# The head of a linear-attention and MLP kernel: the first key weight chunk loaded ahead of the second tile of tokens, and the first tile started alone

## The chip, the cores and the metric

The kernel runs on one core of a Trainium2 chip. A core has TensorE (PE, matrix products; PEld is its loading of weights), VectorE (DVE), ScalarE (ACT), GpSimd (POOL) and SyncE (SP, here a queue that issues DMA transfers), each with its own stream of instructions, in order, and semaphores between them. On-chip memory is SBUF, 128 partitions wide; TensorE writes its results into PSUM. The metric is the time of one execution in microseconds on the device, lower is better. Before the change the median of 3 runs is 414.81 us (414.78 to 414.87).

## The reference

Tokens x (2048 rows, 512 wide, float32) are normalised per row and go through two branches that are added to x:

```python
xn = _layernorm(x, axis=-1)
return x + _A_ref(xn, A_wqkv, A_wo) + _B_ref(xn, B_w1, B_b1, B_w2, B_b2)
```

Branch A is linear attention with 32 heads of 16: q, k and v are `xn @ wqkv`; `phi(t)` is `t + 1` above 0 and `exp(t)` below, plus 1e-6; per head `kv = phi(k)^T v` and `z = sum phi(k)`; the output is `(phi(q) kv) / (phi(q) z + 1e-6)`, times `wo`. Branch B is `relu(xn w1 + b1)^2 w2 + b2` with 1376 hidden units. The row normalisation is

```python
m = jnp.mean(x, axis=axis, keepdims=True)
v = jnp.var(x, axis=axis, keepdims=True)
return (x - m) / jnp.sqrt(v + eps)
```

The change touches only this normalisation and the key product `xn @ wk` of the first two tiles.

## The kernel before

The 2048 tokens are 16 tiles of 128. A float32 product is made of three passes: each operand is split into a high part (`h`, rounded) and a low part (`l`, the rest), and high by high, low by high and high by low are added in PSUM. The key weights `wk` are four chunks of 128 rows (`rk` as loaded, `wk[0]` high, `wk[1]` low), so the keys of a tile take 4 x 3 = 12 products of 128x512. For the first two tiles these products stand in an order written out by hand, since tokens and weights are still arriving.

A tile goes through these steps:

- `load_x` (line 159): its tokens by DMA on SP.
- `measure` (lines 230, 231): two DVE operations give mean and variance.
- `roots`: DVE adds eps to the variance (line 241), POOL raises it to the power -0.5 (line 242).
- `normalise`: DVE subtracts the mean and multiplies by the root, giving `xp` (line 264).
- `transposed` / `turned_pe`: four TensorE turns (line 304) into PSUM, as two halves of two chunks each for tiles 0 and 1. `high()` then has ScalarE round a half into `xs1h` (line 320), and `low()` has DVE subtract that from the PSUM half, giving `xs1l` (line 323). Behind the turns, POOL's memset (line 342) writes 1 into the last column of `xp`.
- `some(i, u, js)` (line 365) issues the products of tile i's part u (0 high, 1 low) with the high parts of weight chunks js, and `rest(j)` those of both tiles' high parts with the low part of chunk j.
- Later `phi_k` makes phi of the keys (lines 356 to 360), `tokens` splits the normalised tokens (ScalarE, then POOL at line 119), `parts` splits the keys (ScalarE, then DVE at line 373), and `kx` (line 385) multiplies the two and adds into four PSUM banks over all tiles.

`heads_k(j)` copies chunk j of the key weights on ScalarE to its high part (line 111, `wkh`), and `rests_k(engine, j)` subtracts that from the chunk on DVE or POOL (line 559, `wkl`). POOL does chunk 1, DVE chunks 0, 2 and 3.

No planner orders this. The program is written under a manual schedule: every engine does its instructions in the order of the Python text, and waits at each for what it needs. So moving a line moves its instruction past others of its own engine. SP's queue holds, in this order, tile 0, tile 1, the four key chunks, tiles 2 and 3 (one transfer), and tiles 4 to 7 (`x4`, one transfer). The last is held back by a small POOL copy out of `xp` of tile 1 into `x4` (line 586). Eleven products of zeros run on TensorE while the first loads are under way.

Behind the head the work is a steady alternation of keys (12 products of line 365), turns (4) and `kx` (12 products of line 385), and then the products of queries, attention and the MLP by tiles of the hidden units.

Of the kernel before, what the change touches and what calls it, by code (L numbers as in the profile page):

```python
# [10 lines left out]
OP = mybir.AluOpType  # L11
# [7 lines left out]
def kernel(  # L19
# [30 lines left out]
    nc = tc.nc  # L50
# [5 lines left out]
    NJ = D // P  # L56
# [24 lines left out]
    def w512(name, tag, bufs):  # L81
        return work.tile([P, 512], F32, name=name, tag=tag, bufs=bufs)
# [8 lines left out]
    def two(name):  # L91
        return keep.tile([P, 2, 512], F32, name=name, tag=next_tag("x"))

    def four(name, tag, dt=F32, pool=None):
        return (pool or work).tile([P, TB, 512], dt, name=name, tag=tag)
# [4 lines left out]
    def f32(ap):  # L100
        return ap.bitcast(F32)

    def gjc(ap):

        return ap.rearrange("p (j g c) -> p g j c", j=NJ, g=NJ)
# [3 lines left out]
    def copy(eng, o, i, bias=0.0):  # L109
        if eng == "act":  # L110
            nc.scalar.activation(o, i, AF.Copy, bias=bias)  # L111
        elif bias:
            ENG[eng].tensor_scalar(o, i, bias, None, op0=OP.add)
        else:
            ENG[eng].tensor_copy(o, i)
# [41 lines left out]
    def load_x(i, t):  # L157
        n = t.shape[1]
        nc.sync.dma_start(t, xf[i * P:(i + n) * P, :].rearrange("(i p) d -> p i d", i=n))
        for k in range(n):  # L160
            xr[i + k] = t[:, k]
# [6 lines left out]
    def chunk(w, j, a, b):  # L168

        return w[j * P:(j + 1) * P, a:b]  # L170
# [52 lines left out]
    def group(*tiles):  # L223
        return tiles, *(small.tile([P, 3, k], F32, name=f"{n}{tiles[0]}", tag=n) for n, k in (("st", 6), ("mv", 2), ("y", 3)))

    def measure(g, *ks):

        tiles, st, mv, _ = g
        for k in ks or range(len(tiles)):
            nc.vector.bn_stats(st[:, k, :], xr[tiles[k]])  # L230
            nc.vector.bn_aggr(mv[:, k, :], st[:, k, :])

    def statistics(*tiles):
        g = group(*tiles)
        measure(g)
        return g

    def roots(tiles, st, mv, y):

        n = len(tiles)  # L240
        nc.vector.tensor_scalar(y[:, 1, :n], mv[:, :n, 1], 1e-5, None, op0=OP.add)
        nc.gpsimd.tensor_tensor(out=y[:, 0, :n], in0=y[:, 1, :n], in1=power[:, :n], op=OP.pow)  # L242

    def normalise(tiles, st, mv, y):

        n = len(tiles)
        r, u = (y[:, k, :n] for k in range(2))
        if tiles[-1] >= NPE:

            nc.vector.scalar_tensor_tensor(u, mv[:, :n, 0], -1.0, r, op0=OP.mult, op1=OP.mult)  # L250
        later = []

        def last(i, o, src, k):
            nc.scalar.activation(o, src, AF.Identity, bias=u[:, k:k + 1], scale=r[:, k:k + 1])
            if i in groups:
                regroup(i)

        for k, i in enumerate(tiles):
            o, src = xp[i], xr[i]
            if i >= NDVE:  # L260

                o, src = o.rearrange("p g (j c) -> p g j c", j=NJ), gjc(src)
            if i < NPE:
                nc.vector.tensor_scalar(o, src, mv[:, k, 0:1], r[:, k:k + 1], op0=OP.subtract, op1=OP.mult)
                if i in groups:
                    regroup(i)
            else:
                later.append(lambda a=(i, o, src, k): last(*a))
        return later
# [3 lines left out]
    def regroup(i):  # L273

        src, G = groups[i]
        via = dram.tile([P, NJ, src.shape[-1]], F32, name=f"via{i}")
        nc.sync.dma_start(via, src)
        of_g = via.rearrange("(r t) g n -> g t r n", r=NJ)
        for g in range(NJ):
            moves.append((G[32 * g:32 * (g + 1)], of_g[g]))  # L280
# [6 lines left out]
    def turn(o, G):  # L287

        nc.vector.transpose(o.rearrange("p j (r t) -> p r j t", r=NJ),
                            G.rearrange("p r (j c) -> p r j c", j=NJ))  # L290

    def slot(i):
        return slice((i % TB) * P, (i % TB + 1) * P)

    def cols(i):

        return xsb[(i // TB + 1) % 2]

    def turned_pe(i, n=1):

        t = [bank(f"pt{i}{k}", "acc" if i < 3 else "ps")[:, :D // n] for k in range(n)]
        for j in range(NJ):
            k, at = divmod(j * P, D // n)
            nc.tensor.transpose(t[k][:, at:at + P], xp[i][:, j * P:(j + 1) * P], ident)  # L304
        ones(i)
        return [p.rearrange("p (j t) -> p j t", j=NJ // n) for p in t]

    def transposed(i, n=1):

        b, at = i // TB, slot(i)  # L310
        if i < NDVE:
            t = turned_pe(i, n)
        else:
            t = [xT[b][:, :, at] if i >= NPE else w512(f"t{i}", "p", 6).rearrange("p (j t) -> p j t", j=NJ)]
            turn(t[0], xg[i])
        m = NJ // n
        h, l = ([x[:, k * m:(k + 1) * m, at] for k in range(n)] for x in cols(i))

        def high(k=0):
            nc.scalar.activation(h[k], t[k], AF.Copy)  # L320

        def low(k=0):
            nc.vector.tensor_tensor(out=l[k], in0=t[k], in1=f32(h[k]), op=OP.subtract)

        def keep_t():
            o = t[0]
            if i < NDVE:
                o = w512(f"t{i}", "p", 6).rearrange("p (j t) -> p j t", j=NJ)
                for k in range(n):
                    copy("act", o[:, k * m:(k + 1) * m], t[k])  # L330
            if i < NPE:
                nc.sync.dma_start(xTd[b][:, :, at], o)

        return high, low, keep_t
# [27 lines left out]
    def project(i, ps, w, steps, first=True, last=True):  # L362

        for n, (j, u, v) in enumerate(steps):
            nc.tensor.matmul(ps, lhsT=cols(i)[u][:, j, slot(i)], rhs=w[v][:, j, :], start=first and n == 0,  # L365
                             stop=last and n == len(steps) - 1)
# [147 lines left out]
    for _ in range(WARM):  # L514
        nc.tensor.matmul(pw[:, :P], lhsT=zeros, rhs=zeros, start=True, stop=True)
    t, rk = two("x0"), four("rk", "r0")
    for i in range(2):
        load_x(i, t[:, i:i + 1])
    def load_k(*js):
        for j in js:  # L520
            nc.sync.dma_start(rk[:, j], chunk(wqkv, j, D, 2 * D))

    load_k(*range(NJ))
    load_x(2, two("x2"))
    nc.gpsimd.memset(power, -0.5)
    nc.gpsimd.memset(ident, 0.0)
# [10 lines left out]
    for i0 in range(0, NT, TB):  # L537
# [5 lines left out]
        n = TB if i0 >= NPE else NPE - NDVE  # L543
        o = work.tile([P, n, 512], F32, name=f"xg{i0}", tag="r0" if i0 + TB == NT else "r3" if i0 >= NPE else "rc")
        for k in range(0, n, 2):
            i = i0 + TB - n + k
            u, v = (t.rearrange("p a (g c) -> p (a g c)", g=NJ) for t in (a[:, TB - n + k:][:, :2], o[:, k:k + 2]))
            groups[i + 1] = [t.rearrange("p (g n) -> p g n", g=NJ) for t in (u, v)]
            u, v = (t.rearrange("p (g i c) -> p g i c", g=NJ, i=2) for t in (u, v))
# [3 lines left out]
    def heads_k(*js, eng="act"):  # L553
        for j in js:
            copy(eng, wk[0][:, j, :], rk[:, j])

    def rests_k(eng, *js):
        for j in js:
            ENG[eng].tensor_tensor(out=wk[1][:, j, :], in0=rk[:, j], in1=f32(wk[0][:, j, :]), op=OP.subtract)
# [3 lines left out]
    def some(i, u, js, first=False):  # L563
        project(i, pks[i], wk, [(j, u, 0) for j in js], first, False)

    def rest(j):
        for i in range(2):
            project(i, pks[i], wk, [(j, 0, 1)], False, j == NJ - 1)

    two_tiles = group(0), group(1)  # L570
    for t in two_tiles:
        measure(t)
        roots(*t)
    normalise(*two_tiles[0])
    heads_k(0)
    high, low, keep0 = transposed(0, 2)
    normalise(*two_tiles[1])
    high1, low1, keep1 = transposed(1, 2)
    high()
    rests_k("dve", 0)  # L580
    some(0, 0, (0,), True)
    high1()
    low()
    some(0, 1, (0,))

    nc.gpsimd.tensor_copy(x4[:, 0, :1], xp[1][:, :1])
    load_x(4, x4)
    low1()
    some(1, 0, (0,), True)
    some(1, 1, (0,))  # L590
    rest(0)
    heads_k(1)
    rests_k("pool", 1)
    high(1)
    some(0, 0, (1,))
    some(0, 1, (1,))
    some(1, 0, (1,))
    some(1, 1, (1,))
    high1(1)
    rest(1)  # L600
    heads_k(2, 3)
    low(1)
    low1(1)
    third = statistics(2)
    roots(*third)
    rests_k("dve", 2)
    for j in (2, 3):
        for i in range(2):
            for u in range(2):
                some(i, u, (j,))  # L610
    normalise(*third)
    keep0()
    keep1()
# [2 lines left out]
    high, low, keep2 = transposed(2)  # L616
    high()
    low()
    rest(2)
    rest(3)  # L620
    load_x(8, x8[:, :2])
# [8 lines left out]
    parts(0)  # L630
    keep2()
    roots(*fourth)
    normalise(*fourth)
    phi_k(1, pks[1])
# [142 lines left out]
    for i in range(2, NT):  # L777
# [9 lines left out]
        high = low = keep_t = lambda: None  # L787
        if i + 1 < NDVE:
            high, low, keep_t = transposed(i + 1)
# [109 lines left out]
    for n in range(2):  # L899
# [339 lines left out]
        for e, f in enumerate(waiting[:-2]):  # L1239
# [14 lines left out]
            if n == 0 and 1 <= e < 5:  # L1254
                k, u = divmod(e - 1, 2)
# [68 lines left out]
```

## Time and profile before

| | |
|---|---|
| median of 3 runs | 414.81 us (414.78 to 414.87) |
| profiled execution, its own time | 414.74 us |
| span in the profile | 413.0 us |
| granted TensorE clock | 1.00 |
| TensorE busy | 407.2 us, 99% |
| VectorE busy | 311.9 us, 76% |
| ScalarE busy | 265.8 us, 64% |
| GpSimd busy | 55.8 us, 14% |
| TensorE busy from 0 to 8.93 us | 6.48 us |
| TensorE busy from 8.93 to 12.57 us | 3.64 us |
| TensorE busy from 12.57 to 20.20 us | 7.52 us |

A row of the timeline gives start, duration, engine, line, operation, the tile written and the tiles read, shapes, and in brackets how long the engine had been idle and what ended that. `x2` at the end of a row means that several instructions are merged, and the duration is theirs together. All times count from the start of the span. A row with `x` is the raw tokens, `xp` the normalised, `pt` the turned tokens in PSUM, `rk`, `wkh` and `wkl` the key weights, `pk` the keys, `y` the variance and its root, and `mv` the mean and variance. In the view of waits a row gives who waited for whom, the sum in us, how often, and the longest.

### The profile page before, as it was taken

The page shows a single profiled execution, that of the slowest core. Times are in us where ns is not written, and L with a number is a line of the kernel's source. Part 1 is how long each engine was busy: PE and PEld are TensorE (multiplying, and loading weights), DVE is VectorE, ACT ScalarE, POOL GpSimd, SP SyncE. Part 2 cuts the span into 40 slices and gives each one's busy share as a digit, 9 for nine tenths or more (in the row PEclk, how much of TensorE's full clock was granted, in tenths as well). Part 3 has the DMA queues.
Part 4 walks back from the last instruction along what each step waited for, and adds up shares of the span by engine and source line. Part 5 has one row for each costly group of instructions (what it writes and reads, how often), then busy time and mean ns, then how long its engine had stood idle before and what let it go on. Part 6 is the DMA issues. An engine that isn't in the chain of part 4 may idle for free.

```text
span 413.0 us, 5389 instructions
## 1 busy us (share of the span) xinstructions
PE 407.2 (99%) x1835; PEld 336.7 (82%) x1835; DVE 311.9 (76%) x563; ACT 265.8 (64%) x467; POOL 55.8 (14%) x81
## 2 busy tenths in 40 slices
PE   7999999999999999999999999999999999999996
PEld 6788888888888888888878888888888888878885
DVE  5795666798799898998439996468989685449843
ACT  4667667756678789788547631567588857737420
POOL 4442333220320000020000040100000200000310
PEclk9999999999999999999999999999999999999999
DMA  6889572710322312264267992411121781024502
GB/s 222 297 242 358 196 238 102 232 51 2 103 75 55 100 51 70 85 188 67 102 244 247 378 202 76 127 52 51 53 76 27 226 185 48 2 87 166 103 1 102
DMA packets 44925, 54.62 MB, mean 132 GB/s; under 512 B 7905, under 2 KB 29153, under 8 KB 43618
## 3 DMA queue, kind: packets, MB, share of 16 engines
q1 hardware_dynamic: 42594, 50.09, 36.9%
q0 software_dynamic: 2304, 4.20, 6.5%
q8 instruction: 14, 0.23, 0.2%
q14 instruction: 13, 0.11, 0.1%
HBM read 41.16 MB, written 13.11 MB: 131 GB/s over the span
## 4 chain that ended last, share of the span: by engine, by line
PE 96%; DVE 2%; DMA 1%; ACT 0%; POOL 0%; issue 0%
PE acc L130 37%; PE b L484 32%; PE kx L385 10%; PE pk L365 10%; PE acc L495 2%; PE pz L130 1%; PE pkv L875 1%; PE pm L130 1%; DMA x<-in_A_x_dram 1%; PE pz0b L130 1%; PE b L130 1%; DVE st L230 0%; POOL y L242 0%; PE acc L502 0%; PE pt L304 0%; DVE k L360 0%
## 5 line engine op out<-in xcount | busy, mean ns | idle before, releaser
L130 PE MATMUL acc<-w2r,s 128*128 128x512 f32 x477 | 112.8, 390 | 0.0
L130 PEld LDWEIGHTS acc<-w2r,s 128*128 128x128 f32 x477 | 89.5, 188 | 19.2 <-issue 0.7
L484 PE MATMUL b<-T,aop 128*128 128x512 f32 x336 | 83.4, 390 | 0.0
L484 PEld LDWEIGHTS b<-T,aop 128*128 128x128 f32 x336 | 63.1, 188 | 13.1
L385 PE MATMUL kx<-pk,tok 128*128 128x512 f32 x192 | 46.5, 392 | 0.1
L385 PEld LDWEIGHTS kx<-pk,tok 128*128 128x128 f32 x192 | 35.8, 188 | 7.7 <-ACT pk L111 0.4
L1005 POOL DMA_DIRECT2D res<-in_B_b_dram x16 | 14.2, 1069 | 182.6 <-DVE dt L426 64.7
L484 PE MATMUL b<-xs0h,aop 128*128 128x512 f32 x112 | 36.9, 391 | 0.0
L130 PE MATMUL acc<-mh,aTsr 128*128 128x512 f32 x112 | 35.7, 390 | 0.0
L1013 DVE TENSOR_TENSOR res<-acc,res 128x512 f32<-128x512 f32 x16 | 11.0, 692 | 23.1 <-PE acc L130 18.5
L119 POOL TENSOR_TENSOR tok<-xp,tok 128x512 fp32r<-128x512 f32 x16 | 20.8, 1303 | 43.5 <-ACT tok L111 43.5
L122 DVE TENSOR_TENSOR w2r<-r,w2r 128x512 fp32r<-128x512 f32 (+2 forms) x35 | 25.6, 734 | 0.1
L130 PEld LDWEIGHTS acc<-mh,aTsr 128*128 128x128 f32 x112 | 21.0, 188 | 4.4
L484 PEld LDWEIGHTS b<-xs0h,aop 128*128 128x128 f32 x112 | 21.0, 188 | 4.3
L111 ACT ACTIVATE aop<-S 128x512 fp32r<-128x512 f32 x28 | 17.5, 624 | 10.6 <-DVE S L704 10.6
L119 DVE TENSOR_TENSOR aop<-S,aop 128x512 fp32r<-128x512 f32 x28 | 19.5, 698 | 4.8 <-ACT aop L111 4.4
L119 DVE TENSOR_TENSOR s<-c,s 128x512 fp32r<-128x512 f32 x20 | 13.6, 690 | 11.5 <-ACT s L111 11.4
L484 PE MATMUL b<-xs0l,aop 128*128 128x512 f32 x56 | 21.8, 390 | 0.0
L130 PE MATMUL acc<-ml,aTsr 128*128 128x512 f32 x56 | 21.8, 390 | 0.0
L111 ACT ACTIVATE w2r<-r 128x512 fp32r<-128x512 f32 x32 | 19.6, 618 | 2.4 <-DMA out_dram<-res 2.0
L111 ACT ACTIVATE T<-Tf 128x512 fp32r<-128x512 f32 x16 | 9.5, 626 | 16.6 <-DVE Tf L647 16.5
L484 PE MATMUL b<-xs1h,aop 128*128 128x512 f32 x56 | 19.5, 390 | 0.0
(194 smaller groups left out, 768.3 us busy)
## 6 DMA issues: line engine op xcount, KB each, us to landing
r<-in_B_w_dram SPq DMA_DIRECT2D x49, 256.0 KB, 3.0
res<-in_A_x_dram SPq DMA_DIRECT2D x8, 512.0 KB, 4.6
res<-in_B_b_dram POOLq DMA_DIRECT2D x16, 256.0 KB, 5.7
out_dram<-res SPq DMA_DIRECT2D x15, 256.0 KB, 2.1
x<-in_A_x_dram SPq DMA_DIRECT2D x5, 512.0 KB, 5.8
via<-xp SPq DMA_DIRECT2D x5, 512.0 KB, 2.7
xg<-via SPq DMA_DIRECT2D x20, 128.0 KB, 2.9
xTd<-t SPq DMA_DIRECT2D x8, 256.0 KB, 3.5
```

The source lines that it names most:

```text
L111: nc.scalar.activation(o, i, AF.Copy, bias=bias)
L119: ENG[el].tensor_tensor(out=l, in0=src, in1=f32(h), op=OP.subtract)
L122: nc.vector.tensor_tensor(out=l, in0=src, in1=f32(h), op=OP.subtract)
L130: nc.tensor.matmul(ps, lhsT=a[u], rhs=b[v], start=first and n == 0, stop=last and n == 2)
L365: nc.tensor.matmul(ps, lhsT=cols(i)[u][:, j, slot(i)], rhs=w[v][:, j, :], start=first and n == 0, stop=last and n == len(steps) - 1)
L385: nc.tensor.matmul(kxp[c], lhsT=tok[i][:, u, c * P:(c + 1) * P], rhs=pk[i][:, v], start=i == 0 and (u, v) == first, stop=i == NT - 1 and ( ...
L484: nc.tensor.matmul(ps, lhsT=a[u][:, j * P:(j + 1) * P], rhs=b[v][:, j, :], start=first and j == 0 and n == 0, stop=last and j == 1 and n == 2,
L495: nc.tensor.matmul(ps, lhsT=s[u][:, k * P:(k + 1) * P], rhs=w2s[NF - 1][u][:, a:z], start=first and u == 0, stop=stop and u == 1)
L875: nc.tensor.matmul(ps[:, at], lhsT=wvs[:, c, at], rhs=kxs[c // 2][:, c % 2, at], start=c == 0 and j == 0, stop=c == NJ - 1 and j == NJ - 1 ...
L1005: nc.gpsimd.dma_start(r[:, i], b2[None, :].partition_broadcast(P), accum_op=OP.add)
L1013: nc.vector.tensor_tensor(out=r[:, a:z], in0=ps, in1=r[:, a:z], op=OP.add)
```

## The change

Three things change, all in the first two tiles but for the first.

- `roots` does its add of eps on POOL, for all groups of tiles, right in front of the power that POOL does anyway.
- SP's queue loads tile 0, key chunk 0, tile 1, key chunks 1 to 3.
- Tile 0 is measured, normalised, turned and multiplied by chunks 0 and 1 first. Tile 1 is measured behind `xp` of tile 0, normalised and turned behind tile 0's first four products. POOL's rest of chunk 1 stands right behind tile 1's root, and DVE's rest of chunk 0 right behind tile 1's `xp`. `rest` takes the tiles it is for, so the products with the low parts of chunk 0 are issued per tile. The number of products stays.

```diff
     def roots(tiles, st, mv, y):
         n = len(tiles)
-        nc.vector.tensor_scalar(y[:, 1, :n], mv[:, :n, 1], 1e-5, None, op0=OP.add)
+        nc.gpsimd.tensor_scalar(y[:, 1, :n], mv[:, :n, 1], 1e-5, None, op0=OP.add)
...
-    for i in range(2):
-        load_x(i, t[:, i:i + 1])
...
-    load_k(*range(NJ))
+    load_x(0, t[:, :1])
+    load_k(0)
+    load_x(1, t[:, 1:])
+    load_k(*range(1, NJ))
     load_x(2, two("x2"))
...
-    def rest(j):
-        for i in range(2):
+    def rest(j, *tiles):
+        for i in tiles or range(2):
             project(i, pks[i], wk, [(j, 0, 1)], False, j == NJ - 1)
 
     two_tiles = group(0), group(1)
-    for t in two_tiles:
-        measure(t)
-        roots(*t)
+    measure(two_tiles[0])
+    roots(*two_tiles[0])
     normalise(*two_tiles[0])
     heads_k(0)
     high, low, keep0 = transposed(0, 2)
+    high()
+    measure(two_tiles[1])
+    roots(*two_tiles[1])
+    some(0, 0, (0,), True)
+    low()
+    heads_k(1)
+    some(0, 1, (0,))
+    some(0, 0, (1,))
+    some(0, 1, (1,))
     normalise(*two_tiles[1])
+    rests_k("pool", 1)
     high1, low1, keep1 = transposed(1, 2)
-    high()
-    rests_k("dve", 0)
-    some(0, 0, (0,), True)
-    high1()
-    low()
-    some(0, 1, (0,))
 
     nc.gpsimd.tensor_copy(x4[:, 0, :1], xp[1][:, :1])
     load_x(4, x4)
+    rests_k("dve", 0)
+    high(1)
+    heads_k(2)
+    high1()
+    low(1)
     low1()
+    high1(1)
+    heads_k(3)
+    low1(1)
+    some(0, 0, (2,))
+    rest(0, 0)
     some(1, 0, (0,), True)
-    some(1, 1, (0,))
-    rest(0)
-    heads_k(1)
-    rests_k("pool", 1)
-    high(1)
-    some(0, 0, (1,))
-    some(0, 1, (1,))
+    rest(0, 1)
+    rest(1)
+    some(0, 1, (2,))
     some(1, 0, (1,))
-    some(1, 1, (1,))
-    high1(1)
-    rest(1)
-    heads_k(2, 3)
-    low(1)
-    low1(1)
+    some(1, 1, (0, 1))
     third = statistics(2)
     roots(*third)
     rests_k("dve", 2)
-    for j in (2, 3):
-        for i in range(2):
-            for u in range(2):
-                some(i, u, (j,))
+    some(1, 0, (2,))
+    some(1, 1, (2,))
+    for i in range(2):
+        for u in range(2):
+            some(i, u, (3,))
     normalise(*third)
```

## The prediction

> **What bounds the kernel now.** I read the page first.
>
> ```profile
> span 413.0 us, 5389 instructions
> PE 407.2 (99%) x1835; PEld 336.7 (82%) x1835; DVE 311.9 (76%) x563; ACT 265.8 (64%) x467; POOL 55.8 (14%) x81
> ```
>
> TensorE is busy 99% of the span, so time is made or lost only where TensorE waits. The view of waits, for TensorE's weight loads, says where (columns: us in total, times, longest).
>
> ```profile
> PEld pt L304 <- DVE xp L264: 2.0, 2, 1.4
> PEld kx L385 <- ACT pk L111: 0.4, 1, 0.4
> PEld pk L365 <- DVE xs1l L323: 0.4, 1, 0.4
> ```
>
> All three lie before 21 us; no later wait on another engine tops 0.1 us. A shift at 21 us is therefore a shift of the end. Third, the timeline of the head: start, duration, engine, line.
>
> ```profile
> 1.71 1.85 SPq L521 DMA_DIRECT2D rk<-in_A_wqkv_dram  x4
> 3.58 0.69 DVE L230 BATCH_NORM_STATS2 st<-x 128x6 f32<-128x512 f32 x1 [3.58 <-DMA x<-in_A_x_dram]
> 4.30 0.18 DVE L231 BATCH_NORM_AGGREGATE mv<-st 128x2 f32<-128x6 f32 x1
> 4.52 0.15 DVE L241 TENSOR_SCALAR y<-mv 128x1 f32<-128x1 f32 x1
> 4.59 0.68 DVE L230 BATCH_NORM_STATS2 st<-x 128x6 f32<-128x512 f32 x1
> 4.76 0.57 POOL L242 TENSOR_TENSOR y<-y,power 128x1 f32<-128x1 f32 x1 [2.36 <-DVE y L241]
> 5.60 0.54 DVE L264 TENSOR_SCALAR xp<-x,mv,y 128x512 f32<-128x512 f32 x1
> 5.76 0.80 POOL L242 TENSOR_TENSOR y<-y,power 128x1 f32<-128x1 f32 x1 [0.43 <-DVE y L241]
> 6.19 0.66 PE L304 MATMUL pt<-ident,xp 128*128 128x128 f32 x4 [1.21 <-DVE xp L264]
> 6.20 0.63 ACT L111 ACTIVATE wkh<-rk 128x512 fp32r<-128x512 f32 x1 [4.12 <-DMA rk<-in_A_wqkv_dram]
> 6.59 0.55 DVE L264 TENSOR_SCALAR xp<-x,mv,y 128x512 f32<-128x512 f32 x1 [0.46 <-POOL y L242]
> 7.05 0.69 DVE L559 TENSOR_TENSOR wkl<-rk,wkh 128x512 fp32r<-128x512 f32 x1
> 7.19 0.66 PE L304 MATMUL pt<-ident,xp 128*128 128x128 f32 x4 [0.35 <-DVE xp L264]
> 7.61 0.47 PE L365 MATMUL pk<-wkh,xs1h 128*128 128x512 f32 x1
> 7.65 0.86 DVE L323 TENSOR_TENSOR xs1l<-pt,xs1h 128x256 fp32r<-128x256 f32 x2
> 7.67 0.38 ACT L320 ACTIVATE xs1h<-pt 128x256 fp32r<-128x256 f32 x1 [0.57 <-PE pt L304]
> 8.65 1.31 POOL L559 TENSOR_TENSOR wkl<-rk,wkh 128x512 fp32r<-128x512 f32 x1 [0.51 <-ACT wkh L111]
> 8.93 0.62 PE L365 MATMUL pk<-wkl,xs1h 128*128 128x512 f32 x2
> 9.55 0.69 DVE L230 BATCH_NORM_STATS2 st<-x 128x6 f32<-128x512 f32 x1
> 10.57 0.69 DVE L559 TENSOR_TENSOR wkl<-rk,wkh 128x512 fp32r<-128x512 f32 x1
> 10.72 0.95 POOL L242 TENSOR_TENSOR y<-y,power 128x1 f32<-128x1 f32 x1 [0.76 <-DVE y L241]
> 11.70 0.55 DVE L264 TENSOR_SCALAR xp<-x,mv,y 128x512 f32<-128x512 f32 x1 [0.44 <-POOL y L242]
> 12.57 0.60 PE L304 MATMUL pt<-ident,xp 128*128 128x128 f32 x4
> ```
>
> Now: statistics of both tiles, turns of tile 0 (6.19) and tile 1 (7.19), the first product at 7.61. The fifth product starts at 8.93, the sixth 0.23 later at 9.16, and from there TensorE runs without a gap to the turns of tile 2 at 12.57. One more gap is left, the 0.4 us ahead of `kx` of tile 1.
>
> **What two engines do to each other.** The change brings VectorE (DVE) and GpSimd (POOL) work on SBUF side by side, so I looked for such pairs.
>
> ```profile
> 15.77 1.29 POOL L119 TENSOR_TENSOR tok<-xp,tok 128x512 fp32r<-128x512 f32 x1 [2.44 <-ACT tok L111]
> 16.62 0.99 DVE L373 SCALAR_TENSOR_TENSOR pk<-k,pk 128x512 fp32r<-128x512 f32 x1
> 18.35 0.55 DVE L264 TENSOR_SCALAR xp<-x,mv,y 128x512 f32<-128x512 f32 x1 [0.67 <-POOL y L242]
> 20.23 0.66 DVE L373 SCALAR_TENSOR_TENSOR pk<-k,pk 128x512 fp32r<-128x512 f32 x1
> 30.14 1.30 POOL L119 TENSOR_TENSOR tok<-xp,tok 128x512 fp32r<-128x512 f32 x1 [2.12 <-ACT tok L111]
> 30.64 0.82 DVE L241 TENSOR_SCALAR y<-mv 128x2 f32<-128x2 f32 x1
> ```
>
> The L373 operation, 0.66 us alone, takes 0.99 when POOL is at work until 15.77 + 1.29 = 17.06, and ends 0.55 after that. An L241 add, 0.15 at 4.52, takes 0.82 and ends at 31.46, just behind POOL's 31.44. The other way: the power, 0.57 alone, takes 0.95 beside `wkl` (to 11.26) and ends 0.41 behind it; beside `xp` (to 6.14) it takes 0.80 and ends 0.42 behind. So the second one stands still, some 0.14 us after its start, until the first is done. [...]
>
> **The change part by part.** *Load order.* Key chunk 0 goes from the third place of SP's queue to the second, tile 1 the other way. Second place had landed by 4.59 (its statistics start then, waiting for nothing), third by 6.20. So the copy of chunk 0 moves from 6.20 to about 4.6 and is hidden until 6.5. Tile 1 lands between 4.6 and 6.2.
>
> ```profile
> DMA to landing us min/median/max: 4.5/4.8/5.0
> x<-in_A_x_dram SPq DMA_DIRECT2D x1, 1024.0 KB, 4.9
> ```
>
> The key chunks, issued 0.46 apart, land 4.5 to 5.0 later (first row), so about 0.65 apart. I take one such step behind 4.6, so 5.3; 6.2 would cost 0.28, below.
>
> *The add on POOL.* Ten adds leave DVE (the group's row below). Those of tiles 0 to 3 are costed here; for the other six, in the stretch without gaps, TensorE never waits: nothing, and without that cover about 0.3 each. An add on POOL has no row. Two small POOL rows bound it:
>
> ```profile
> L241 DVE TENSOR_SCALAR y<-mv x10: 124/161/822, 4.5 to 66.8; 128x1 f32<-128x1 f32 x5, 128x2 f32<-128x2 f32 x4, 128x3 f32<-128x3 f32 x1
> ...
> 1.12 0.29 POOL L527 TENSOR_SCALAR_AFFINE_SELECT ident<-ident 128x128 f32<-128x128 f32 x1
> 7.96 0.18 POOL L586 COPY x<-xp 128x1 f32<-128x1 f32 x1
> ```
>
> The copy of one column, 0.18, is below; the one-column power, 0.57, is the far end above. I take 0.20, near the copy, whose shape it has; the affine row has 128 columns in 0.29.
>
> *Tile 0 alone.* Its mean ends at 4.30 + 0.18 = 4.48; plus 0.09 to POOL (4.67 to 4.76), add 0.20, 0.09 again, power 0.57: 5.43. Normalised from 5.46 (was 5.60, behind tile 1's statistics), turned from 5.46 + 0.59 = 6.05, first half rounded by 6.05 + 0.48 + 0.38 = 6.91, first product at 6.96 (was 7.61). Its low half and chunk 1 (landing about 7.0: issued at 2.17, plus 4.8; 0.63 to round) give products 2 to 4 at 7.44, 7.68 and 7.91. TensorE is free at about 8.13 with four products done. Before, the same work (less tile 1's turns, 0.42) was done at 8.93. So far this is a gain.
>
> *Tile 1 behind it.* Its statistics follow `xp` of tile 0 by 0.46 (6.59 to 7.05): 5.92, done 0.90 later (3.58 to 4.48) at 6.82; add 6.91, power 7.20 to 7.77. Now three operations of the standing-still kind meet: POOL's `wkl` chunk 1 (1.31), which the new order puts right behind the power; DVE's `xp` of tile 1 (0.55) and `wkl` chunk 0 (0.69). In the old order POOL's came at 8.65, after both. POOL first: 7.77 + 1.31 = 9.08, `xp` done 0.40 behind at 9.48, turns 9.53, fifth product 9.95, `wkl` done at 10.08, sixth product (it needs `wkl` chunk 0) at 10.18. DVE first: `xp` 7.80 to 8.35, turns 8.40, POOL 1.17 behind at 9.52, `wkl` 0.55 behind at 10.07, sixth product at 10.12. Either way 10.15 against 9.16: **+0.99**. Queued behind on DVE are the low halves, behind on POOL only the memset and the copy that frees tile 4's load. That load goes out about 2.2 later (10.2 for 8.1), lands 4.9 later (second row of the landings above) at 15.1, and is wanted at about 17. ScalarE's copies of chunks 1 to 3 now stand between its halves, and the order of the products changes but not their number: nothing, while DVE and POOL are the late ones; 0.6 for each copy if they are not.
>
> [...]
>
> *Tile 2.* Behind `wkl` (10.08) DVE has three low halves (two took 0.86 at 7.65, and a start can lie 0.08 ahead of the end before it, as 7.65 is to 7.74), so tile 2's statistics start at about 11.1 (were 9.55). From there to `xp` it was 11.70 - 9.55 = 2.15, power and `wkl` chunk 2 side by side; now the add too stands behind that `wkl`: +0.15, less 0.08 for the add gone from DVE. Taking 2.25, `xp` is at 13.35 and the turns at 13.94 (+0.59). TensorE would be there at 10.15 + (12.57 - 9.16) = 13.56: **+0.38**, between 0 (statistics in time) and 0.6.
>
> *Tile 3.* The `kx` gap hangs on `xp` at 18.35, behind power and add. The add on POOL stands behind L373, which ends at 17.61; add and power then end near 18.27 in the old clock, not 18.32: **-0.07**, between -0.4 (the whole gap, were the add ahead of L373) and +0.1.
>
> Sum: 0.99 + 0.38 - 0.07 = +1.30. The profiled execution took 414.74, beside its span of 413.0; the median of the runs is 414.81, so the two differ by less than anything here. 414.74 + 1.30 = 416.0.
>
> **The rivals.** *DVE has both its turns first* (ends on the other side: no measurable change). If `xp` and `wkl` chunk 0 both run ahead of POOL, `wkl` chunk 0 is done at 8.95, POOL's at 8.95 + 1.15 = 10.1, and only the ninth product (9.84 before) waits, to 10.15: +0.3, and tile 2 is in time: 415.0. [...] Chance 0.13. *No standing still at all*: the fifth product is at 8.80 instead of 8.93, tile 2 is in time, and the `kx` gap shrinks by 0.3: -0.4, 414.3. Three pairs of rows speak against it. Chance 0.07. *The add is dear*: at 0.57 tile 0 is no earlier (5.83 for 5.60: the change doesn't do what it says) and tile 1 pays twice, 0.74 more: 416.8. The affine row speaks against it. Chance 0.15. Late tokens of tile 1 (6.2) belong to the main case: 416.3.
>
> **How the numbers follow.** Main case 0.62, its own range 415.6 to 416.5. Beside it and the rivals 0.03 is left for what I don't see. The range 414.9 to 416.9 holds the main case, the dear add and DVE-first, and leaves out no standing still and the tails. 0.2% is 0.83 us, about what a measurement here can tell from no change: slower from 415.64. Slower: 0.60 of the main case and the dear add, 0.75; same: DVE-first, the rest of the main case and most of the no-stall case, 0.21; faster 0.04.
>
> **What would show it.** Right: first product near 6.96; then a TensorE wait of over 1 us ahead of the turns of tile 1 or of the sixth product; either `xp` of tile 1 near 1.7 us or `wkl` chunk 0 near 1.8, ending 0.40 or 0.55 behind POOL's `wkl`; turns of tile 2 near 13.9. Wrong: `xp` and `wkl` at 0.55 and 0.69 with POOL's beside them; the sixth product before 9.3; a POOL add over 0.3; or a wait behind 21 us that was not there.

## The result, and the profile after

The changed kernel takes 416.38 us (median of 6 runs, 416.06 to 416.73) against 414.79 (6 runs, 414.73 to 414.87): ratio 1.0039, 95% interval 1.0028 to 1.0049. It is 1.6 us slower, and the forecast of 416.0 lies 0.4 under it. The profiled execution took 416.41, 1.67 more than that of before.

The page of the changed kernel, its first lines:

```profile
span 414.7 us, 5393 instructions
PE 408.9 (99%) x1835; PEld 337.4 (81%) x1835; DVE 311.1 (75%) x553; ACT 266.2 (64%) x467; POOL 58.6 (14%) x91
```

Ten operations left VectorE and ten came to GpSimd, as the diff says, and TensorE does the same 1835 products and turns. The waits of TensorE's weight loads, in the changed kernel:

```profile
PEld pt L304 <- DVE xp L264: 1.9, 2, 1.4
PEld pk L365 <- ACT xs1h L320: 0.6, 2, 0.4
PEld pt L304 <- issue: 0.5, 1, 0.5
PEld kx L385 <- ACT pk L111: 0.4, 1, 0.4
PEld pk L365 <- DVE xs1l L323: 0.3, 1, 0.3
```

The wait for `xp` is no longer that of the start: its longest, 1.4, now stands in the middle of the products, ahead of the turns of tile 1. I count the `issue` row as a wait too: it stands ahead of the turns of tile 2, whose first weight load comes at 14.13, 0.11 behind the end of tile 2's `xp` (13.47 + 0.55). The timeline of the changed kernel (start, duration, engine):

```profile
5.49 0.55 DVE L264 TENSOR_SCALAR xp<-x,mv,y 128x512 f32<-128x512 f32 x1 [1.03 <-POOL y L242]
6.09 0.97 PE L304 MATMUL pt<-ident,xp 128*128 128x128 f32 x4 [0.22 <-DVE xp L264]
6.67 0.18 DVE L231 BATCH_NORM_AGGREGATE mv<-st 128x2 f32<-128x6 f32 x1
7.12 0.10 POOL L342 MEMSET xp<- 128x1 f32 x1 [1.67 <-PE pt L304]
7.18 0.23 POOL L241 TENSOR_SCALAR y<-mv 128x1 f32<-128x1 f32 x1
7.25 0.49 PE L365 MATMUL pk<-wkh,xs1h 128*128 128x512 f32 x1 [0.20 <-ACT xs1h L320]
7.50 0.58 POOL L242 TENSOR_TENSOR y<-y,power 128x1 f32<-128x1 f32 x1
8.05 1.27 POOL L560 TENSOR_TENSOR wkl<-rk,wkh 128x512 fp32r<-128x512 f32 x1
8.12 1.49 DVE L264 TENSOR_SCALAR xp<-x,mv,y 128x512 f32<-128x512 f32 x1 [0.46 <-POOL y L242]
8.28 0.40 PE L365 MATMUL pk<-wkh,xs1l 128*128 128x512 f32 x1
9.52 0.68 DVE L560 TENSOR_TENSOR wkl<-rk,wkh 128x512 fp32r<-128x512 f32 x1
9.66 0.66 PE L304 MATMUL pt<-ident,xp 128*128 128x128 f32 x4 [0.98 <-DVE xp L264]
10.39 0.39 PE L365 MATMUL pk<-wkl,xs1h 128*128 128x512 f32 x1
12.04 0.66 DVE L560 TENSOR_TENSOR wkl<-rk,wkh 128x512 fp32r<-128x512 f32 x1
12.22 0.57 POOL L241 TENSOR_SCALAR y<-mv 128x1 f32<-128x1 f32 x1 [1.61 <-DVE mv L231]
12.87 0.57 POOL L242 TENSOR_TENSOR y<-y,power 128x1 f32<-128x1 f32 x1
13.47 0.55 DVE L264 TENSOR_SCALAR xp<-x,mv,y 128x512 f32<-128x512 f32 x1 [0.77 <-POOL y L242]
14.16 0.63 PE L304 MATMUL pt<-ident,xp 128*128 128x128 f32 x4
18.25 0.98 DVE L373 SCALAR_TENSOR_TENSOR pk<-k,pk 128x512 fp32r<-128x512 f32 x1
18.64 0.67 POOL L241 TENSOR_SCALAR y<-mv 128x1 f32<-128x1 f32 x1
19.40 0.58 POOL L242 TENSOR_TENSOR y<-y,power 128x1 f32<-128x1 f32 x1
20.01 0.55 DVE L264 TENSOR_SCALAR xp<-x,mv,y 128x512 f32<-128x512 f32 x1 [0.78 <-POOL y L242]
```

Read it downward. Tile 0 is normalised at 5.49, and its first product comes at 7.25 (before: 7.61). Four products start by 8.28. Then GpSimd's `wkl` (8.05 to 9.32) and VectorE's `xp` of tile 1 (from 8.12) meet, and `xp` takes 1.49 instead of 0.55. TensorE stands from 8.68 to 9.66 (the 0.98 of that row). The sixth product is at 10.39 against 9.16 (+1.23), the turns of tile 2 at 14.16 against 12.57 (+1.59). From there to the end hardly anything is added: `kx` of tile 1, in the chain that ended last (start, duration), before and in the changed kernel, is 1.66 later, and the whole execution 1.67.

```profile
20.21 3.02 PE kx L385 x12
21.87 3.01 PE kx L385 x12
```

### The profile page after: what moved, and what is told of

The parts are those of the page before. It is cut to its first block, busy times and chain, and to the rows that moved or that the text cites. A ratio compares the mean times of both kernels' runs of the same rounds, so it can differ in the third digit from the quotient of the medians.

```text
span 414.7 us, 5393 instructions
## 1 busy us (share of the span) xinstructions
PE 408.9 (99%) x1835; PEld 337.4 (81%) x1835; DVE 311.1 (75%) x553; ACT 266.2 (64%) x467; POOL 58.6 (14%) x91
## 4 chain that ended last, share of the span: by engine, by line
PE 96%; DVE 1%; POOL 1%; DMA 1%; ACT 1%; issue 0%; POOLq 0%
PE acc L130 37%; PE b L484 32%; PE kx L385 10%; PE pk L365 10%; PE acc L495 2%; PE pz L130 1%; PE pkv L881 1%; PE pt L304 1%; PE pm L130 1%; DMA x<-in_A_x_dram 1%; PE pz0b L130 1%; PE b L130 1%; DVE xp L264 1%; POOL y L242 0%; PE acc L502 0%; POOL tok L119 0%
## 5 line engine op out<-in xcount | busy, mean ns | idle before, releaser
L119 POOL TENSOR_TENSOR tok<-xp,tok 128x512 fp32r<-128x512 f32 x16 | 21.1, 1319 | 41.8 <-ACT tok L111 41.8
L119 DVE TENSOR_TENSOR aop<-S,aop 128x512 fp32r<-128x512 f32 x28 | 19.5, 698 | 4.8 <-ACT aop L111 4.4
L119 DVE TENSOR_TENSOR s<-c,s 128x512 fp32r<-128x512 f32 x20 | 13.6, 690 | 11.5 <-ACT s L111 11.4
```

Of the source, the lines that this page charges most:

```text
L119: ENG[el].tensor_tensor(out=l, in0=src, in1=f32(h), op=OP.subtract)
```

## The experiments

**GpSimd's rest of chunk 1 late (from the changed kernel).**

```diff
     normalise(*two_tiles[1])
-    rests_k("pool", 1)
     high1, low1, keep1 = transposed(1, 2)
...
     load_x(4, x4)
+    rests_k("pool", 1)
     rests_k("dve", 0)
...
     rest(0, 1)
-    rest(1)
     some(0, 1, (2,))
...
     some(1, 1, (2,))
+    rest(1)
```

> GpSimd's rest of weight chunk 1 moved behind the copy that frees tile 4's load (so behind tile 1's turns), and the two products that need it moved behind chunk 2's products. Theory (GpSimd's 1.3 us operation holds a resource that tile 1's normalisation needs): xp of tile 1 back from 1.49 to about 0.55 us, tile 1's turns at about 8.7 instead of 9.66, sixth product near 9.4 instead of 10.39, turns of tile 2 near 13.2 instead of 14.16; median near 415.4. Rival (the loss is the serial order itself: add, power, normalise, turn of tile 1 one behind the other): turns of tile 1 stay at 9.4 or later, median 416.2 or more.

Measured 415.33 us (10 runs; ratio to before 1.0014, 1.0004 to 1.0023). The timeline of this kernel:

```profile
8.03 0.55 DVE L264 TENSOR_SCALAR xp<-x,mv,y 128x512 f32<-128x512 f32 x1 [0.47 <-POOL y L242]
8.63 0.66 PE L304 MATMUL pt<-ident,xp 128*128 128x128 f32 x4
9.36 0.40 PE L365 MATMUL pk<-wkl,xs1h 128*128 128x512 f32 x1
9.53 1.29 POOL L560 TENSOR_TENSOR wkl<-rk,wkh 128x512 fp32r<-128x512 f32 x1
```

`xp` is back at 0.55, the turns of tile 1 are 1.03 earlier, the sixth product is at 9.36. One operation moved on another engine, with the two products that need it, brings 1.05 us of the 1.6 back. The serial order of tile 1 stayed as it was, so it is not what cost them.

**The same operation in two halves (from the changed kernel).**

```diff
-    rests_k("pool", 1)
+    for c in range(2):
+        at = slice(c * 256, (c + 1) * 256)
+        nc.gpsimd.tensor_tensor(out=wk[1][:, 1, at], in0=rk[:, 1, at], in1=f32(wk[0][:, 1, at]), op=OP.subtract)
```

> GpSimd's rest of chunk 1 as two operations of half the width. Theory of the held resource: tile 1's xp waits for the first half only, so it takes about 0.9 instead of 1.49 us and tile 1's turns come 0.6 earlier, near 9.05; the second half then gets in between and holds VectorE's rest of chunk 0, which takes about 1.2 us, so the sixth product is only 0.1 to 0.3 earlier; median near 416.2. Rival (a fixed cost that does not depend on what GpSimd does): xp stays at 1.49.

Measured 416.41 us (4 runs; 1.0038, 1.0023 to 1.0053). The timeline of this kernel, where the first row is both halves together:

```profile
8.35 1.60 POOL L589 TENSOR_TENSOR wkl<-rk,wkh 128x256 fp32r<-128x256 f32 x2
8.42 0.94 DVE L264 TENSOR_SCALAR xp<-x,mv,y 128x512 f32<-128x512 f32 x1 [0.71 <-POOL y L242]
9.29 1.21 DVE L560 TENSOR_TENSOR wkl<-rk,wkh 128x512 fp32r<-128x512 f32 x1
10.56 0.50 PE L365 MATMUL pk<-wkl,xs1h 128*128 128x512 f32 x1 [0.25 <-DVE wkl L560]
```

This is the sharpest test. `xp` falls from 1.49 to 0.94 and `wkl` of chunk 0 rises from 0.68 to 1.21, both as forecast: here the wait went with the width of the other engine's operation. The two halves ran from 8.35 to 9.95, 1.60 together against 1.27 for the one operation. `xp` ended at 9.36, 0.59 before they were through, and `wkl` of chunk 0 at 10.50, 0.55 behind them. So in this run `xp` did not wait for both halves, only `wkl` did. That the engines took turns, first half, `xp`, second half, `wkl`, is my reading of these times: the row does not part the halves. The turns of tile 1, expected near 9.05, came at 9.42, since tile 1's power was late in this execution (7.80 against 7.50). Its statistics would have started at about 6.47 against 5.95 (an estimate: 1.33 ahead of the power, as tile 0's in the changed kernel, 3.54 and 4.87). The total is not better: from tile 1's power (7.80 here, 7.50 before this edit) to the sixth product it is 2.76 instead of 2.89, a gain of 0.13 that this execution lost to a later power. Here cutting the operation in two only moved the wait.

**The add of eps back on VectorE (from the changed kernel).**

```diff
-        nc.gpsimd.tensor_scalar(y[:, 1, :n], mv[:, :n, 1], 1e-5, None, op0=OP.add)
+        nc.vector.tensor_scalar(y[:, 1, :n], mv[:, :n, 1], 1e-5, None, op0=OP.add)
```

> The changed kernel with the add of eps back on VectorE. Theory (the add on GpSimd costs its 0.23 us and a handover on tile 1's path, and stands behind VectorE's weight rest on tile 2's and tile 3's): power of tile 1 0.3 earlier, turns of tile 2 some 0.4 earlier, gap before tile 1's kx products about 0.1 smaller; median near 415.9. Rival (the power waits for the same things anyway): 416.3 to 416.5.

Measured 415.91 us (7 runs; 1.0036, 1.0019 to 1.0052), 0.47 less than the changed kernel by the medians and as expected. By them about 0.5 of the 1.6 us is the add, but the two intervals (1.0019 to 1.0052, and 1.0028 to 1.0049 for the changed kernel) overlap, so this run alone does not show it. The profiled execution, at 416.20, was one with late statistics of tile 1 (their second operation, L231, at 6.91 against 6.67); counted from there, the turns of tile 2 come 7.13 later instead of 7.49. `xp` of tile 1 still takes 1.64 us here, beside GpSimd's `wkl` (8.04 to 9.32).

**The add alone on GpSimd (from the kernel before).** The same line, the other way.

> The kernel before with nothing changed but the add of eps on GpSimd. Theory: the add costs about 0.3 on tile 1's path (it stands behind xp of tile 0 on VectorE, then goes ahead of the power), little at tile 2 (0.28 of slack there), 0.07 at tile 3: median near 415.1. Rival (an add beside the power is free, and VectorE wins its time): 414.6 to 414.8.

Measured 414.81 us (10 runs; 1.0001, 0.9992 to 1.0010): no difference. My expectation of 0.3 was wrong. The timeline of this kernel shows why nothing is lost at tile 1:

```profile
5.35 0.21 POOL L241 TENSOR_SCALAR y<-mv 128x1 f32<-128x1 f32 x1
5.64 0.73 POOL L242 TENSOR_TENSOR y<-y,power 128x1 f32<-128x1 f32 x1
```

I had tile 1's add standing behind `xp` of tile 0. It began a moment ahead of it (5.35, `xp` at 5.39) and ran its 0.21, and only the power stood still (0.73 instead of the 0.58 of tile 0's). That the slack of 0.28 covers what the add costs at tile 2 is argued and not shown: the profiled execution, at 415.48, was the longest of the ten, and in it tile 2's tokens landed late (statistics at 10.26, 9.55 before). So by the medians the add costs nothing in the old order and about 0.5 in the new one.

**The memset of tile 0 later (from the changed kernel).**

```diff
     roots(*two_tiles[1])
+    ones(0)
...
-        ones(i)
+        if i:
+            ones(i)
```

> The changed kernel with GpSimd's memset of tile 0's last column (it waits for tile 0's turns) moved behind tile 1's add and power. Theory (GpSimd is in order, so tile 1's add waits for TensorE's turns of tile 0): the add starts at about 6.95 instead of 7.18, everything behind 0.2 to 0.25 earlier where tile 0's turns run slow, nothing where they run fast; median near 416.15. Rival (the add is not held by the memset): 416.4, add at 7.18.

Measured 416.28 us (5 runs; 1.0037, 1.0024 to 1.0050). The 0.1 against the changed kernel is less than the spread of either. In this kernel's profile the turns of tile 0 took 0.66, so the memset would not have held the add. What it costs when those turns take 0.97, as in the profile after, is not settled.

**VectorE's rest of chunk 2 late too (from the first experiment).**

```diff
     third = statistics(2)
     roots(*third)
-    rests_k("dve", 2)
...
     normalise(*third)
+    rests_k("dve", 2)
```

> The kernel with GpSimd's rest of chunk 1 late, and VectorE's rest of chunk 2 moved behind tile 2's xp. Theory (tile 2's add and power stand still behind that rest, which costs the gap ahead of tile 2's turns): add 0.23 and power 0.58 at once, no gap ahead of tile 2's turns (13.13 before this edit, about 12.8 with it), 0.36 off 415.33: median near 415.0. Rival (tile 2 is late because of its own statistics): turns of tile 2 at 13.1, median 415.3.

Measured 415.30 us (10 runs; 1.0014, 1.0004 to 1.0023): nothing against 415.33. The timeline of this kernel:

```profile
12.14 0.55 DVE L264 TENSOR_SCALAR xp<-x,mv,y 128x512 f32<-128x512 f32 x1 [0.99 <-POOL y L242]
12.61 1.28 DVE L560 TENSOR_TENSOR wkl<-rk,wkh 128x512 fp32r<-128x512 f32 x2
12.93 0.60 PE L304 MATMUL pt<-ident,xp 128*128 128x128 f32 x4
13.94 0.30 PEld L365 LDWEIGHTS pk<-wkl,xs1h 128*128 128x128 f32 x2 [0.30 <-DVE wkl L560]
```

The gap ahead of the turns of tile 2 did go: they start at 12.93. A new one came behind them, 0.30 at 13.94, where the products of chunks 2 and 3 now wait for the rests that were put off. The mechanism held; I had not asked what the moved operation would be late for.

**The load order alone (from the kernel before).**

```diff
-    for i in range(2):
-        load_x(i, t[:, i:i + 1])
...
-    load_k(*range(NJ))
+    load_x(0, t[:, :1])
+    load_k(0)
+    load_x(1, t[:, 1:])
+    load_k(*range(1, NJ))
```

> The kernel before with nothing changed but the load order. Theory: tile 1's tokens land at 5.2 to 5.8 instead of 4.15, and VectorE, in order, holds tile 0's xp behind tile 1's statistics, so everything is 0.7 to 1.2 later: median 415.4 to 416.0. Rival (the order of 256 KB transfers is hidden): 414.8.

Measured 416.61 us (4 runs, 416.17 to 417.66; 1.0046, 1.0032 to 1.0060): 1.8 more than before, above what I expected. The profiled execution took 416.99. The timeline of this kernel:

```profile
5.55 0.69 DVE L230 BATCH_NORM_STATS2 st<-x 128x6 f32<-128x512 f32 x1 [0.85 <-DMA x<-in_A_x_dram]
7.16 0.66 PE L304 MATMUL pt<-ident,xp 128*128 128x128 f32 x4 [1.80 <-DVE xp L264]
9.51 0.63 PE L365 MATMUL pk<-wkh,xs1l 128*128 128x512 f32 x1
9.93 0.63 PE L365 MATMUL pk<-wkh,xs1h 128*128 128x512 f32 x1
```

And one stretch of it in the view of windows (stretch, length, busy time and count of PE, PEld, DVE, ACT and POOL, then the granted TensorE clock, the share of DMA and GB/s):

```profile
8.40:11.60 3.20, 3.20 (x11) 2.68 (x11) 2.53 (x7) 2.71 (x8) 1.51 (x3) 0.52 0.29 44
```

Tile 1 lands at 5.55, and since VectorE is in order and does both tiles' statistics first, the turns of tile 0 are at 7.16 instead of 6.19: +0.97, as expected. The rest I had not seen: from 8.40 to 11.60 the granted clock is 0.52 and products come every 0.42 instead of 0.23.

**The load order with more products of zeros in front (from the last one).** `WARM = 11` becomes `WARM = 14`.

> The kernel before with the new load order, and 14 products of zeros in front instead of 11, so that TensorE is busy until about 6.8 and idle for less before tile 0's turns at 7.16. Theory (of the 1.8 us that the load order alone cost, about 0.95 is tile 1's late landing and the rest is TensorE running the first products at half pace, 0.427 each, after its idle stretch): the first products at 0.23 each, median near 415.7. Rival (the slow pace has nothing to do with the idle stretch): first products at 0.427 again, median 416.6.

Measured 415.57 us (10 runs, 415.30 to 416.37; 1.0023, 1.0013 to 1.0033), 1.0 less than with eleven. Three rows of its timeline:

```profile
7.75 0.66 PE L304 MATMUL pt<-ident,xp 128*128 128x128 f32 x4 [0.96 <-DVE xp L264]
10.03 0.40 PE L365 MATMUL pk<-wkh,xs1h 128*128 128x512 f32 x1
10.26 0.39 PE L365 MATMUL pk<-wkh,xs1l 128*128 128x512 f32 x1
```

The idle stretch ahead of the turns is 0.96 instead of 1.80, the products are 0.23 apart, and the mean granted clock of the whole execution is 1.00 (0.995 with eleven), although tile 1 landed later still in this execution (its statistics start at 6.14). From these statistics to the end of the span it is 408.5 us here (6.14 to 414.6) and 409.7 with eleven (5.55 to 415.2). So between the two profiled executions the half pace was worth about 1.2 us (an estimate: 409.7 less 408.5). Of the four executions with eleven, two show a mean granted clock of 0.995 and 0.996 and took 416.99 and 417.66, and two show 1.00 and took 416.22 and 416.17; none of the ten with fourteen shows less than 0.998.

**The tile-0-first order mended (from the kernel with both rests late).** The add back on VectorE, and tile 3's root ahead of GpSimd's token split:

```diff
     fourth = statistics(3)
+    roots(*fourth)
...
     keep2()
-    roots(*fourth)
```

> The changed order with everything taken out that the runs so far showed to cost time: GpSimd's rest of chunk 1 late, VectorE's rest of chunk 2 behind tile 2's xp, the add back on VectorE, tile 3's root ahead of GpSimd's token split. Theory (starting tile 0 alone costs nothing by itself; what costs is what it brought side by side): 0.47 (the add, from the run with the add on VectorE) and about 0.3 (the gap ahead of tile 1's kx) off 415.3, so 414.4 to 414.7, no slower than the kernel before. Rival (tile 1 behind tile 0 costs time by itself): 415.0 or more.

Measured 414.44 us (11 runs, 414.03 to 415.47; 0.9993, 0.9984 to 1.0002): no slower than the kernel before, as the theory asked. But tile 3's root, part of this mend, shortens the old order too (to 414.37 in the next experiment), and the old order with all its mends takes 414.10 in the last. So starting tile 0 alone, with its load order, gains nothing, and that it costs up to 0.3 by itself is not excluded. Against the kernel with both rests late the two edits bring 0.86; with 0.45 for the root (next experiment, in the old order) about 0.4 is left for the add, near the 0.5 above.

**Tile 3's root early, alone (from the kernel before).** The last diff alone.

> The kernel before with tile 3's root moved ahead of GpSimd's token split, and nothing else. Theory: the gap ahead of tile 1's kx products (0.28 us of TensorE) goes, median near 414.5, and the other 0.4 of the mended kernel's gain is in its other edits. Rival (tile 1's keys wait for ScalarE's exponential in any case): 414.75.

Measured 414.37 us (11 runs; 0.9989, 0.9980 to 0.9998), 0.45 less than before; the two profiled executions differ by 0.34. In its profile the power of tile 3 has moved into a stretch in which GpSimd is idle (it starts at 14.09, behind 2.27 of idle time, and the token split waits 1.13 more, to 15.82), and the wait ahead of `kx` of tile 1, 0.4 before, is

```profile
PEld kx L385 <- ACT pk L111: 0.2, 1, 0.2
```

**The kernel before with its order mended.**

```diff
     high()
+    low()
     rests_k("dve", 0)
     some(0, 0, (0,), True)
     high1()
-    low()
     some(0, 1, (0,))
...
     some(1, 0, (0,), True)
-    some(1, 1, (0,))
     rest(0)
+    some(1, 1, (0,))
...
     high1(1)
-    rest(1)
...
-    rests_k("dve", 2)
     for j in (2, 3):
         for i in range(2):
             for u in range(2):
                 some(i, u, (j,))
+        if j == 2:
+            rest(1)
     normalise(*third)
+    rests_k("dve", 2)
...
     fourth = statistics(3)
+    roots(*fourth)
...
     keep2()
-    roots(*fourth)
```

> The kernel before, loads and add as they were, with the order mended by what the traces show: low halves of tile 0 ahead of VectorE's rest of chunk 0 and that rest's products ahead of tile 1's low ones; chunk 1's rest products behind chunk 2; VectorE's rest of chunk 2 behind tile 2's xp; tile 3's root ahead of the token split on GpSimd. Theory (each is time on TensorE's path): seventh product at about 9.0 instead of 9.39, turns of tile 2 at about 12.2, no gap ahead of tile 1's kx; median near 414.2. Rival (the head is bound by something else, such as the arrival of chunk 1 and ScalarE's copies): 414.7.

Measured 414.10 us (11 runs, 413.96 to 414.38; 0.9983, 0.9974 to 0.9991). It beats both kernels: 0.7 under the one before and 2.3 under the changed one. Its timeline:

```profile
8.99 0.39 PE L365 MATMUL pk<-wkh,xs1h 128*128 128x512 f32 x1
12.17 0.60 PE L304 MATMUL pt<-ident,xp 128*128 128x128 f32 x4
```

and its waits ahead of TensorE's weight loads:

```profile
PEld pk L365 <- DVE wkl L559: 0.3, 1, 0.3
PEld kx L385 <- ACT pk L111: 0.2, 1, 0.2
```

The seventh product is at 8.99 (9.39 before) and the turns of tile 2 are at 12.17 (12.57). Of each 0.40, 0.15 does not come from the edits: tile 0's tokens landed earlier in this execution (statistics at 3.43 against 3.58). By the run above, 0.45 of the 0.7 is tile 3's root. How the other 0.25 divides among the other edits was not tried.

## Why the prediction was right

The direction, the place and the mechanism held. Behind tile 1's power GpSimd's `wkl` ran first, in 1.27 (1.31 before); `xp` stood still beside it (1.49), and VectorE's `wkl`, queued behind `xp`, came late without standing still (0.68). TensorE's weight loads waited 1.42 for `xp`, TensorE itself 0.98, and the end moved with it. The first two experiments show it: with the operation taken away 1.05 us came back, and with it halved the wait shrank as forecast. Of the two orders that I left open, GpSimd was first.

| step | predicted | profile after |
|---|---|---|
| `xp` of tile 0 starts | 5.46 | 5.49 |
| first product | 6.96 | 7.25 |
| add, end of power, tile 1 | 6.91, 7.77 | 7.18, 8.08 |
| end of GpSimd's `wkl` | 9.08 | 9.32 |
| turns of tile 1 | 9.53 | 9.66 |
| sixth product, against before | 10.15 to 10.18, +0.99 | 10.39, +1.23 |
| tile 2's turns, added | +0.38 | +0.36 |
| tile 3, added | -0.07 | +0.08 |
| sum | +1.30 | +1.67 |

Point by point:

- *The load order.* Tile 1 did land in time for `xp` of tile 0 to be first: its statistics start at 5.95, 0.46 behind, as taken. Later statistics were seen in another execution of this head (the add back on VectorE: L231 at 6.91 against 6.67), and with the two halves tile 1's power was late (7.80 against 7.50), so the late case stays a real part of the spread.
- *The add.* I took 0.20, it is 0.23. The dear add (0.57) fell. Standing behind VectorE's `wkl` at 12.22 it does take 0.57, and that was in the term for tile 2.
- *The front, mis-sized by 0.24.* I took the first half of tile 0's turns as ready 0.48 behind their start, from the row of tile 1's turns in the profile before. It was 0.73 (6.09 to 6.82), since the turns ran slower (0.97 for the four, 0.66 before). And I let the memset on GpSimd pass without asking what it waits for: it waits for those turns, and tile 1's add stands behind it in the queue (7.12, then 7.18, though tile 1's variance is ready at 6.85 and the add could have come 0.09 later). That made the power 0.3 late. `xp` ending 0.29 behind GpSimd's `wkl` instead of 0.40 gave 0.1 back. So the turns of tile 1 were 0.13 late, and the sixth product came 0.19 behind the end of VectorE's `wkl` (10.20) and not 0.10.
- *Tile 3, with the wrong sign, 0.15.* I had add and power end 0.66 behind L373. They ended 0.75 behind it (19.23 to 19.98): the add 0.08 behind L373, a handover of 0.09 that I had counted for tiles 0 and 1 but not here, and the power's 0.58. L373 itself was 0.03 later. The ends that I wrote for the forecast, 18.27 and 18.32, differ by 0.05 and not by the 0.07 of the term; in the same way tile 2's 2.15 + 0.15 - 0.08 is 2.22 where I took 2.25. Neither slip changes the forecast by more than 0.03.
- *The rivals.* VectorE first in both turns, and no standing still, are excluded by the 1.49. That the longer order of tile 1 costs by itself was not among my rivals in the forecast. The mended new order, at 414.44, excludes it as the cause of the 1.6 us; beside the mended old order, at 414.10, up to 0.3 stays open.

The rows show that one operation stands still while the other runs, not which part of the chip the two share. Nor does `xp` need its own whole duration behind `wkl`: 8.05 + 1.27 = 9.32, and `xp` ends at 9.61, 0.29 later, not 0.55. And not every pair of operations shows it: in the profile after, the statistics at 17.43 took 0.68 beside GpSimd's token split (L119, 1.29 at 17.39), about as long as alone (0.69 at 3.54).

## What to carry to other kernels

Before an operation is moved on GpSimd, list what VectorE does at that time: here an operation of 1.27 us that nobody was waiting for drew one of 0.55 us that everybody was waiting for out to 1.49. For each moved instruction ask three things: what it waits for, what stands behind it in its own engine's queue, and what the new place makes late (the second rest of this case cured one wait and made another of the same size). A small chain of operations, mean, add, power, is best issued where its engine is idle: moving one root by a few lines brought 0.45.

## What the runs showed of the hardware that I had not expected

TensorE's pace in the head differs from one execution to the next. The products of zeros in front, in the profile of the kernel before:

```profile
0.84 4.14 PE L515 MATMUL warm<-const-float32-0.0 128*128 128x128 f32 x22 [0.84 <-PEq L1310]
```

and of the changed kernel:

```profile
0.83 5.03 PE L515 MATMUL warm<-const-float32-0.0 128*128 128x128 f32 x22 [0.83 <-PEq L1316]
```

The same 22 records took 4.14 and 5.03, and the turns of tile 0 behind them 0.66 and 0.97. The granted clock is 1.00 over all four of these stretches, so it does not tell them apart, and in the first experiment, whose head is the same up to there, the turns took 0.66. In the profiled execution with the load order alone the granted clock was 0.52 from 8.40 to 11.60, behind an idle stretch of 1.80 us, the turns of tile 0 (0.66) and 0.35 idle; by the estimate above that cost about 1.2 us. With three more products of zeros and 0.96 idle the products came 0.23 apart, not 0.42. That the idle time is the cause rests on these two runs alone. That the old order hides such differences better, since its turns of tile 0 stand before a wait for ScalarE, is argued and not shown.
